# Attention with capped scores, then a two-way maxout layer, on one core: another hand-written order of the same steps, with three buffers for the exponentials instead of two

## The chip, the cores and the metric

The kernel runs on one core of one Trainium2 chip. The metric is the device time of one execution, in microseconds (us). TensorE (PE in the profile), ScalarE (ACT), VectorE (DVE), GpSimd (POOL) and SyncE (SP) each work through a queue of their own in order and wait for one another by semaphores. In this kernel POOL issues the loads that change type on the way, SP issues the transposing transfers and nearly all stores.

## The reference, cut to what matters

```python
# q, k, v: (8 batches, 12 heads, 448 rows, 64), float32; cap = 30
scores = scale * q @ k.T
scores = cap * tanh(scores / cap)
attn = exp(scores - max) / sum
x = (attn @ v), heads side by side        # (3584, 768)
out = maximum(x @ w1, x @ w2) @ w_out     # w1, w2: (768, 1024), w_out: (1024, 768)
```

The maximum is never taken directly: the kernel writes max(a, b) = b + relu(a - b), so with wd = w1 - w2 and wm = w2 @ w_out it computes out = x @ wm + relu(x @ wd) @ w_out.

## The kernel before, in words

**Tiles.** Two neighbouring heads of one batch are a pair of heads; there are 48 of them, and two of these make a *tile* t (0 to 23), four heads. An *item* n is what the attention works on at a time: a tile's 448 queries; tile 2 is cut in two (256 and 192 queries, items 2 and 3), so there are 25 items, and from tile 3 on item n is tile n - 1.

**The order is written out.** `ORDER` (line 10) is a string of 1911 steps. The kernel goes through it from first to last and issues what each step names (the table `STEPS`, line 686 on); every engine gets its share of the steps in that order. No planner decides at run time. A dependency between engines is a wait, which the framework derives from the tiles, so an engine runs ahead of the string wherever its own inputs allow. The steps that this document speaks of:

- `lk`, `lq`, `lv`, `lw1`, `lw2`, `lwo`: one load each on POOL's queue (of keys, queries, values, weights). Keys and queries of a tile go into one of four buffers `kqs`, values into one of four `vp` and `vl`.
- `X`, `XC`: for the first ten pairs of heads, TensorE transposes keys and queries and VectorE copies them to `qkT`. `cr t` does it for tiles 5 and up by one transposing transfer on SP's queue. `qkT` has three buffers, so a transfer also waits until an earlier tile's scores have been computed.
- `S n s z`: scores of item n, part s (0 to 5, 128 keys of two heads each), two matmuls into the score bank pair z (0 or 1). `L n z`: the scores of the 64 keys left over, eight matmuls. `T`, `TL`: tanh on ScalarE, from the bank pair to the exponentials' buffer. `E`: exp in place over two or three parts.
- `A`, `B`: VectorE adds up the exponentials; `Y`: TensorE sums them over the partitions; `Yi`: three VectorE steps to the reciprocal.
- `VL n z`, `V n u`: values times exponentials (8 and 12 matmuls, into bank pair z); `N`: VectorE normalizes into `xT`.
- `O g b` gives group g of the dense layers the bank b; `M x y c` makes c steps of it. With two different groups, a step is two matmuls of 64 rows each that run side by side on the two halves of the array (one half of x, the other half of y); with x = y it is one matmul of 128 rows; with -1 one half stands empty. Groups 0 to 11 are wm, the others belong to batches 0 to 7 in order. `H g` hands the bank from one half to the other by way of VectorE; `ev g` empties the bank to SBUF; `st` stores a block of the output. `sub` makes wd from w1 and w2 on VectorE.
- `D`: matmuls of a constant that nobody uses, which occupy TensorE at the start.

**The buffers of the exponentials.** An item has two tiles of them, one of 6 x 448 columns (`e0`) and one of 8 x 448 (`e1`). `exps_of` (lines 404 to 411) takes each from a pool of `EB` buffers, `EB = 2`. The tanh of item n + 2 can thus start only when the values and sums of item n have been read.

Places that the prediction uses: the first steps of `ORDER`; `lw1 2`, the last part of w1, and `sub 4`, which waits for it; `lv 2 1`, the second half of the values of tile 2; the transfers `cr 17` and `cr 20`; and the last item, 24, after which only dense groups 118 to 139 are left.

Of the kernel before, what the change touches and what calls it, by code (L numbers as in the profile page):

```python
# [14 lines left out]
lv 1 2; lq 6 0; lv 2 2; lw2 1; VL 0 1; W 2 2; WC 2; W 3 3; ev 1; WC 3; D 0 8; lq 5 0; E 0 1 0 2; E 0 0 0 3; Y 0 0;
Yi 0 1; Yi 0 2; Yi 0 3; lv 0 1; lv 0 0; lv 1 0; V 0 0; V 0 1; N 0 0; N 0 1; T 1 0; E 1 0 0 3; S 2 0 0; T 2 0;
E 1 1 2 4; E 1 1 0 2; O 2 2; O 3 1; M 2 3 8; H 3; H 2; lw2 2; W 4 3; WC 4; W 5 0; WC 5; M 3 2 3; lv 3 3; lk 5 0;
X 5 3; M 3 2 5; XC 5; S 2 1 0; lw1 0; sub 1 0; ev 3; L 2 1; TL 2; T 2 1; Y 1 0; Yi 1 1; Yi 1 2; sub 0 0; S 2 2 1;
T 2 2; E 2 1 0 2; O 4 3; O 5 1; M 4 5 8; H 5; lv 1 3; lv 1 1; VL 1 0; V 1 0; V 1 1; S 3 1 1; T 3 1; H 4; M 5 4 1;
ev 2; Yi 1 3; N 1 0; N 1 1; M 5 4 5; E 2 1 2 4; M 5 4 2; ev 5; S 3 0 1; T 3 0; lv 2 1; lq 8 0; lwo 1 0; O 6 0; O 7 2;  # L20
M 6 7 3; lk 6 0; M 6 7 1; lwo 1 1; M 6 7 2; S 3 2 0; T 3 2; M 6 7 2; H 7; H 6; ev 4; X 6 1; XC 6; L 3 1; TL 3;
E 3 1 0 2; lw1 1; sub 3 0; lk 10 0; lk 7 0; lv 3 2; lv 2 3; lv 2 0; lq 7 0; lk 8 0; lw1 2; lk 10 1; lq 10 0; lk 11 0;
lk 9 0; lk 11 1; lq 11 0; cr 5; lv 3 1; lq 9 0; lk 12 0; M 7 6 6; S 4 2 0; T 4 2; M 7 6 2; O 8 3; O 9 1; M 8 9 1;
ev 6; sub 2 0; ev 7; S 4 0 1; T 4 0; M 8 9 7; H 8; H 9; S 4 1 0; T 4 1; E 4 0 0 3; Y 2 0; Yi 2 1; Yi 2 2; VL 2 1;
X 7 2; XC 7; lk 12 1; lq 12 0; lk 13 0; lk 13 1; lq 13 0; lv 4 0; lv 4 1; lv 4 2; lv 4 3; lk 14 0; lv 3 0; lk 14 1;
lq 14 0; lk 15 0; lk 15 1; lq 15 0; X 8 0; XC 8; Yi 2 3; V 2 0; V 2 1; N 2 0; N 2 1; S 4 3 0; T 4 3; E 3 1 2 4;
M 9 8 8; ev 8; O 10 2; O 11 0; M 10 11 2; S 4 5 0; T 4 5; S 4 4 1; T 4 4; sub 5 0; M 10 11 6; H 11; H 10; sub 4 0;
ev 9; Y 3 3; Yi 3 1; S 5 2 0; T 5 2; M 11 10 4; S 5 0 1; T 5 0; M 11 10 4; Yi 3 2; ev 11; ev 10; L 4 0; TL 4; cr 6;
X 9 1; S 5 1 1; T 5 1; E 4 1 0 2; O 13 3; M 13 -1 2; O 14 0; M 13 14 4; O 17 2; M 17 14 2; XC 9; S 5 4 0; H 13;
M 17 13 3; H 14; M 17 13 1; M 14 13 2; VL 3 1; V 3 0; V 3 1; T 5 4; lv 5 0; lv 5 1; lv 5 2; lv 5 3; lk 16 0; lk 16 1;  # L30
lq 16 0; lk 17 0; lk 17 1; lq 17 0; lv 6 0; lv 6 1; lv 6 2; lv 6 3; lk 18 0; A 4 0 1; A 4 0 2; H 17; M 14 17 4; ev 13;
Yi 3 3; N 3 0; O 15 1; M 15 17 2; ev 17; O 19 3; M 15 19 4; H 15; N 3 1; E 4 1 2 4; L 5 0; TL 5; O 12 2; M 12 19 2;
H 19; M 12 15 4; H 12; M 19 15 2; ev 14; ev 15; A 4 1 1; S 5 3 1; T 5 3; E 5 1 0 2; M 19 12 4; ev 19; M -1 12 1;
O 18 0; M 18 12 1; O 16 1; M 18 16 5; H 18; M -1 16 1; H 16; S 5 5 0; cr 7; T 5 5; E 5 0 0 3; ev 12; M -1 18 1;
M 16 18 5; O 22 3; M 16 22 1; O 20 2; M 20 22 9; A 4 1 2; ev 18; B 4 0; B 4 1; L 6 1; VL 4 0; ev 16; A 5 1 1; Y 4 0;
Yi 4 1; Yi 4 2; Yi 4 3; V 4 0; V 4 1; TL 6; lk 18 1; lq 18 0; lk 19 0; lk 19 1; lq 19 0; lv 7 0; lv 7 1; lv 7 2;
lv 7 3; lk 20 0; M 20 22 4; H 22; O 21 1; M 20 21 1; H 20; M -1 21 1; N 4 0; N 4 1; M 22 21 4; A 5 0 1; S 6 5 1; cr 8;
M 22 21 8; H 21; S 6 1 0; M 22 20 2; M 21 20 2; E 5 1 2 4; A 5 1 2; A 5 0 2; ev 22; B 5 1; B 5 0; T 6 5; T 6 1;
S 6 4 1; T 6 4; M 21 20 4; S 6 0 0; T 6 0; E 6 1 2 4; M 21 20 6; ev 20; O 26 0; M 21 26 2; O 27 3; M 27 26 4; H 26;
S 6 2 1; S 6 3 0; T 6 2; T 6 3; E 6 0 0 3; ev 21; st 0 0; O 25 2; M 27 25 2; H 27; M 26 25 4; H 25; M 26 27 2; ev 26;  # L40
M 25 27 4; ev 27; O 29 1; M 25 29 2; ev 25; O 30 0; M 30 29 4; H 29; VL 5 1; Y 5 3; O 24 2; M 30 24 2; M 29 24 3;
S 7 5 0; M 29 24 1; H 30; M 29 30 2; V 5 0; V 5 1; T 7 5; lk 20 1; lq 20 0; lk 21 0; lk 21 1; lq 21 0; lv 8 0; lv 8 1;
lv 8 2; lv 8 3; lk 22 0; lk 22 1; lq 22 0; lk 23 0; lk 23 1; lq 23 0; Yi 5 1; Yi 5 2; Yi 5 3; H 24; M 24 30 3; ev 29;
N 5 0; M 24 30 1; ev 30; M 24 -1 1; O 31 3; M 24 31 1; O 28 1; M 28 31 1; ev 24; M 28 31 4; M 28 -1 1; H 28; H 31;
# [118 lines left out]
def kernel(  # L163
# [572 lines left out]
```

## Time and profile before

| what | us |
|---|---|
| three runs: median (lowest to highest) | 328.62 (328.51 to 330.5) |
| the profiled execution, its own time | 329.16 |
| its span, first to last instruction | 327.4 |
| TensorE busy | 319.1 |
| ScalarE busy | 274.5 |
| VectorE busy | 244.7 |
| GpSimd busy | 163.5 |

Busy time counts an engine's instructions, overlaps once. 1.76 us of the profiled execution lie outside of its span. In lines of the profile, `64*128` is a matmul on 64 rows and 128 columns of the array, `x24` a number of instructions, and a bracket is idle time of the engine just ahead, with what ended it.

### The profile page before, as it was taken

The numbers are of one execution on the slowest core, as the hardware profiler recorded it, in microseconds if no ns is written. First come the engines' busy times: TensorE is split into PE (matmuls) and PEld (weight loads), VectorE is DVE, ScalarE is ACT, GpSimd is POOL, SyncE is SP. The second block draws the span as 40 slices with busy tenths as digits, with TensorE's granted clock in tenths as the row PEclk, the third lists the DMA queues.
The fourth block names the chain that finished last, engine by engine and source line by source line (L and its number), as shares of the span: only waits on it lengthen the run. The fifth ranks groups of instructions, "written<-read, shape, count | busy, mean of one in ns | idle before, by whom it ended". The sixth has DMA issues, their size and how long they took to land.

```text
span 327.4 us, 10010 instructions
## 1 busy us (share of the span) xinstructions
PE 319.1 (97%) x4288; PEld 194.0 (59%) x4288; DVE 244.7 (75%) x447; ACT 274.5 (84%) x245; POOL 163.5 (50%) x241
## 2 busy tenths in 40 slices
PE   7799999999999999999999999999999999999995
PEld 7465567665546656555565565675567568555552
DVE  2349898988888688978888678889788777886213
ACT  3999999999999999999999998999899988900000
POOL 7567589998995865565577387543202000000000
PEclk9899999999999999999999999999999999999999
DMA  8999999999999999999999999996963006003034
GB/s 201 197 230 253 271 159 171 156 175 186 165 161 126 207 139 111 188 190 90 149 152 185 165 191 172 131 75 101 203 150 46 2 0 194 3 2 94 4 96 144
DMA packets 135083, 46.13 MB, mean 141 GB/s; under 512 B 116224, under 2 KB 130688, under 8 KB 134656
## 3 DMA queue, kind: packets, MB, share of 16 engines
q0 software_dynamic: 95168, 24.85, 76.9%
q1 hardware_dynamic: 39184, 19.40, 27.9%
q10 hardware_dynamic: 688, 1.25, 1.1%
q8 instruction: 33, 0.54, 0.7%
q14 instruction: 10, 0.08, 0.1%
HBM read 47.45 MB, written 11.01 MB: 179 GB/s over the span
## 4 chain that ended last, share of the span: by engine, by line
PE 94%; ACT 3%; DVE 2%; issue 0%; DVEq 0%
PE mm L582 59%; PE s L438 9%; PE s L539 9%; PE mm L577 8%; ACT e L447 2%; PE s L456 2%; PE s L529 2%; PE mm L502 2%; PE mm L336 2%; PE mm L365 1%; PE mm L497 1%; ACT e L469 0%; DVE xT L558 0%; PE mm L344 0%; ACT e L462 0%
## 5 line engine op out<-in xcount | busy, mean ns | idle before, releaser
L469 ACT ACTIVATE e<-e 128x1792 bf16<-128x1792 bf16 (+4 forms) x73 | 140.2, 1932 | 0.5
L447 ACT ACTIVATE e<-s 128x896 bf16<-128x896 f32 (+2 forms) x144 | 124.1, 935 | 6.0 <-PE s L438 5.7
L582 PE MATMUL mm<-wo_sb,gT 64*128 64x384 bf16 x768 | 95.8, 323 | 0.0
L582 PE MATMUL mm<-xT,wd_sb 64*128 64x448 bf16 (+2 forms) x768 | 79.9, 326 | 0.0
L582 PE MATMUL mm<-wm_sb,xT 64*128 64x384 bf16 x576 | 77.8, 323 | 0.0
L582 PEld LDWEIGHTS <-gT 64*128 64x128 bf16 x768 | 48.4, 94 | 23.3 <-issue 2.8
L302 POOL DMA_DIRECT2D vp<-in_v_dram x48 | 30.3, 637 | 60.6 <-PE s L539 29.0
L284 POOL DMA_DIRECT2D kqs<-in_k_dram x76 | 54.6, 721 | 9.7 <-DMA qkT<-kqs 3.1
L582 PEld LDWEIGHTS <-wd_sb 64*128 64x128 bf16 x768 | 46.3, 94 | 20.0 <-DVEq L590 2.4
L438 PE MATMUL s<-qkT 64*128 64x448 bf16 (+2 forms) x300 | 53.4, 346 | 2.6 <-ACT e L447 1.7
L582 PEld LDWEIGHTS <-xT 64*128 64x128 bf16 x576 | 38.2, 94 | 17.5 <-issue 2.2
L613 DVE TENSOR_SCALAR gT<-mm 128x448 bf16<-128x448 f32 (+2 forms) x72 | 38.9, 566 | 8.2 <-PE mm L582 4.4
L648 DVE COPY osb<-mm 128x384 f32<-128x384 f32 x54 | 28.4, 551 | 15.8 <-PE mm L577 11.5
L284 POOL DMA_DIRECT2D kqs<-in_q_dram x38 | 35.0, 921 | 1.5 <-DMA vl<-in_v_dram 0.7
L539 PE MATMUL s<-e,vp 128*32 128x448 bf16 (+2 forms) x600 | 32.1, 346 | 0.0
L558 DVE TENSOR_TENSOR xT<-s,inv 64x448 bf16<-64x448 f32 (+2 forms) x50 | 30.2, 603 | 2.4 <-PE mm L582 0.9
L479 DVE TENSOR_TENSOR esum<-esum,e 128x896 bf16<-128x896 bf16 x42 | 25.5, 618 | 7.8 <-PE mm L582 6.9
L438 PEld LDWEIGHTS <-qkT 64*128 64x128 bf16 x300 | 20.2, 94 | 18.6 <-issue 6.8
L302 POOL DMA_DIRECT2D vl<-in_v_dram x48 | 29.4, 622 | 0.3 <-DMA wo_sb<-in_moe_w_out_dram 0.3
L484 DVE TENSOR_TENSOR esum<-esum,e 64x896 bf16<-64x896 bf16 x42 | 26.0, 619 | 3.1 <-PE mm L582 0.8
L479 DVE TENSOR_TENSOR esum<-e 128x896 bf16<-128x896 bf16 x42 | 25.4, 617 | 2.9 <-PE mm L582 1.8
L509 DVE STREAM_TRANSPOSE st<-mm 128x448 f32<-128x448 f32 (+2 forms) x25 | 15.8, 630 | 13.3 <-PE mm L502 10.8
(54 smaller groups left out, 262.1 us busy)
## 6 DMA issues: line engine op xcount, KB each, us to landing
out_dram<-osb SPq DMA_DIRECT2D x51, 192.0 KB, 3.7
vp<-in_v_dram POOLq DMA_DIRECT2D x38, 160.0 KB, 4.9
kqs<-in_q_dram POOLq DMA_DIRECT2D x46, 112.0 KB, 4.9
kqs<-in_k_dram POOLq DMA_DIRECT2D x76, 56.0 KB, 4.3
osb<-in_moe_w_dram POOLq DMA_DIRECT2D x2, 1024.0 KB, 8.3
gT<-in_moe_w_dram POOLq DMA_DIRECT2D x3, 512.0 KB, 7.2
wo_sb<-in_moe_w_out_dram POOLq DMA_DIRECT2D x4, 384.0 KB, 7.0
w1l<-in_moe_w_dram POOLq DMA_DIRECT2D x1, 1024.0 KB, 5.2
```

Of the source, the lines that this page charges most:

```text
L284: nc.gpsimd.dma_start(out=to, in_=x)
L302: nc.gpsimd.dma_start(out=to, in_=x)
L438: nc.tensor.matmul(ps[:, h, x * w : (x + 1) * w], k_of(t, o, h, j), q_of(n, o, h))
L447: nc.scalar.activation(e, slots[n, s][:, :, :m], AF.Tanh, scale=scale / cap)
L469: nc.scalar.activation(e[:, j0 * m : hi], e[:, j0 * m : hi], AF.Exp, scale=float(cap))
L479: nc.vector.tensor_add(d, e[:, 0:2, :] if j == 1 else d, e[:, 2 * j : 2 * j + 2, :])
L539: nc.tensor.matmul(vals[n][R32[m], u, :w], vp[t % VB][:, x, j if turned_by_pe(t) else 2 * j, u::2], e_of(n, o, h, j), start=False, stop=(j ...
L558: nc.vector.tensor_mul(x[to], vals[n][r, 1, :w], sums[n, 3][to, :w])
L577: nc.tensor.matmul(self.ps, w, x, start=first, stop=self.at[0] == self.n)
L582: ins = nc.tensor.matmul(self.ps, w[r], x[r], start=first, stop=self.at == [self.n, self.n]).ins
L613: nc.vector.tensor_relu(gT[b // 2][:, f, cs], ps)
L648: nc.vector.tensor_copy(o[:, hs], ps)
```

## The change

`EB` is 3 instead of 2, and `ORDER` is another string, of 1910 steps. Nothing else differs: every kind of step occurs as often as before, for the same items, groups and loads, but for `M`, whose 1324 steps are cut into 406 pieces instead of 407. Of these steps 1140 are pairs, 160 full and 24 single in both. What differs is the place of nearly every step. The diff, cut to the lines that the prediction speaks of:

```diff
 ORDER = """
-ld0 k; ld0 q; ld1 k; ld1 q; lq 3 0; dm; D 0 32; D 0 8; ms0; cd k; lk 3 0; lw2 0; id; lv 0 3; lv 0 2; cd q; Xh 0 1 0;
-XC 0 1; cd1 q; Xh 0 0 1; XC 0 0; S 0 0 0; T 0 0; S 0 1 1; T 0 1; X 3 2; S 0 2 0; cd1 k; X 1 3; T 0 2; XC 3; S 1 3 1;
...
-ev 2; Yi 1 3; N 1 0; N 1 1; M 5 4 5; E 2 1 2 4; M 5 4 2; ev 5; S 3 0 1; T 3 0; lv 2 1; lq 8 0; lwo 1 0; O 6 0; O 7 2;
...
-M 121 -1 2; ev 121; H 118; ev 123; lv 23 1; lv 23 2; lv 23 3; VL 24 0; V 24 0; Y 24 0; Yi 24 1; Yi 24 2; V 24 1;
...
+ld0 k; ld0 q; ld1 k; dm; D 0 32; ms0; lk 5 0; ld1 q; lq 3 0; lq 4 0; lq 2 0; cd q; cd1 q; cd k; id; Xh 0 0 0; XC 0 0;
+Xh 0 1 1; XC 0 1; S 0 1 0; T 0 1; S 0 0 1; T 0 0; S 0 2 0; T 0 2; E 0 0 0 3; cd1 k; X 1 2; D 3 8; XC 1; S 0 3 1;
+T 0 3; S 0 4 0; T 0 4; E 0 1 0 2; D 3 8; lk 3 0; X 3 3; XC 3; ms; lk 2 0; X 2 0; S 0 5 1; T 0 5; S 1 5 0; T 1 5;
+lw2 0; W 0 1; W 1 2; XC 2; WC 0; L 0 1; TL 0; L 1 0; TL 1; lk 4 0; X 4 3; S 1 1 1; T 1 1; WC 1; lwo 0 0; O 0 0; O 1 1;
...
+sub 3 0; S 4 2 1; T 4 2; E 4 0 0 3; M 9 8 8; ev 8; lk 10 1; lq 8 0; lk 7 0; lk 8 0; X 8 2; XC 8; X 7 0; ev 9; lw1 2;
+sub 4 0; lq 10 0; lk 11 0; lv 2 1; lk 11 1; lq 11 0; cr 5; lk 9 0; lq 9 0; Y 2 3; Yi 2 1; XC 7; S 5 0 0; T 5 0;
+S 5 2 1; T 5 2; O 10 2; O 11 1; M 10 11 8; H 10; Yi 2 2; VL 2 0; V 2 0; V 2 1; H 11; Yi 2 3; N 2 0; N 2 1; A 4 0 1;
...
+lv 15 0; lv 15 1; lv 15 2; S 17 4 0; T 17 4; lv 15 3; lk 36 0; lk 36 1; lq 36 0; lk 37 0; lk 37 1; lq 37 0; cr 18;
+lv 16 0; lv 16 1; lv 16 2; lv 16 3; M 82 74 2; H 75; M 75 74 1; B 16 0; M 75 74 6; cr 17; L 18 1; TL 18; E 17 0 0 3;
...
+lk 41 1; lq 41 0; cr 20; lv 18 0; lv 18 1; lv 18 2; lv 18 3; st 3 4; st 3 5; A 18 0 2; ev 92; lk 42 0; lk 42 1;
...
+O 122 1; M 118 122 2; M 121 122 12; TL 24; E 24 1 2 4; B 24 0; A 24 1 2; VL 24 0; V 24 0; H 118; B 24 1; N 23 1;
...
-    EB = 2
+    EB = 3
```

More of the change, by code (lines that the diff above doesn't have):

```diff
@@ L15 @@
[L15 to L19, printed above, removed]
@@ L20 @@
-ev 2; Yi 1 3; N 1 0; N 1 1; M 5 4 5; E 2 1 2 4; M 5 4 2; ev 5; S 3 0 1; T 3 0; lv 2 1; lq 8 0; lwo 1 0; O 6 0; O 7 2;
[L21 to L44, printed above, removed]
@@ L158 @@
+O 138 1; M 138 138 2; st 7 4; ev 137; ev 136; st 7 5; st 7 3; M 138 138 12; ev 138; O 139 0; M 139 139 14; ev 139;
 st 7 6;
```

251 lines of the change are left out of this document (136 added, 115 removed).

## The prediction

> **What bounds the kernel now.** I read the page first, for the engines' shares, their slices and the chain.
>
> ```profile
> span 327.4 us, 10010 instructions
> ...
> PE 319.1 (97%) x4288; PEld 194.0 (59%) x4288; DVE 244.7 (75%) x447; ACT 274.5 (84%) x245; POOL 163.5 (50%) x241
> ...
> PE   7799999999999999999999999999999999999995
> ...
> ACT  3999999999999999999999998999899988900000
> ...
> DMA  8999999999999999999999999996963006003034
> ...
> PE 94%; ACT 3%; DVE 2%; issue 0%; DVEq 0%
> ```
>
> TensorE is busy 97% of the span and makes up 94% of the chain; ScalarE is nearly as full until slice 36. The reader should see two full engines and a short thin start. Next, the windows by stage (engine busy us, granted clock, DMA):
>
> ```profile
> core 0: us, PE busy (x) PEld busy (x) DVE busy (x) ACT busy (x) POOL busy (x), PEclk, DMA share, GB/s
> 0.00:5.00 5.00, 4.01 (x38) 4.01 (x39) 0.58 (x3) 1.85 (x2) 3.90 (x11) 1.00 0.65 193
> 5.00:10.00 5.00, 3.68 (x97) 2.43 (x94) 2.27 (x5) 3.17 (x5) 3.16 (x6) 1.00 1.21 199
> 10.00:15.00 5.00, 3.54 (x44) 1.75 (x46) 0.69 (x1) 5.00 (x6) 3.77 (x8) 0.81 1.29 201
> 15.00:20.00 5.00, 4.48 (x83) 2.69 (x79) 1.69 (x6) 5.00 (x7) 2.95 (x6) 0.84 1.27 200
> 20.00:26.00 6.00, 5.94 (x98) 4.08 (x100) 4.31 (x8) 5.97 (x4) 4.32 (x8) 1.00 1.15 295
> 26.00:60.00 34.00, 33.91 (x646) 22.05 (x644) 30.55 (x57) 33.50 (x33) 26.52 (x39) 1.00 1.47 201
> ...
> 283.40:327.40 44.00, 40.20 (x338) 22.41 (x338) 22.12 (x41) 2.58 (x3) 0.00 (x0) 1.00 0.22 63
> ```
>
> From 26 to 283 us TensorE is never idle; its idle time lies in the first 20 us (4.3 us of it) and in the last wait for stores. In 10 to 20 us ScalarE has no gap, so there TensorE follows ScalarE. The granted clock is 0.81 and 0.84 there. Then the waits, and two pieces of the timeline: the first score, and a change from one matmul shape to another.
>
> ```profile
> POOL vp L302 <- PE s L539: 29.0, 6, 8.2
> ...
> ACT e L447 <- PE s L438: 5.7, 9, 1.5
> ...
> PE s L438 <- ACT e L447: 1.7, 5, 0.4
> ...
> ACT e L462 <- PE s L539: 0.3, 1, 0.3
> ```
> ```profile
> 5.56 0.83 PEld L365 LDWEIGHTS <-kqs 64*64 64x64 bf16 x28 [0.39 <-issue]
> ...
> 6.99 0.55 PE L438 MATMUL s<-qkT 64*128 64x448 bf16 x4 [0.49 <-DVE qkT L370]
> 7.39 4.96 ACT L447 ACTIVATE e<-s 128x896 bf16<-128x896 f32 x6 [1.54 <-PE s L438]
> ```
> ```profile
> 139.76 0.37 PE L502 MATMUL mm<-esum,ones 128*32 128x448 bf16 x4
> 139.95 1.32 PE L539 MATMUL s<-e,vp 128*32 128x448 bf16 x24
> 141.20 0.33 PE L582 MATMUL mm<-wm_sb,xT 64*128 64x384 bf16 x1
> ```
>
> TensorE waits for ScalarE 1.7 us in all. ScalarE's tanh begins at 7.39 us, and what it waited for is the first score, which waited for a copy to `qkT`, which waited behind filler matmuls: operands were cast by 4.83 us, but the first transpose starts at 5.59. In the last piece, the 24 `V` matmuls start at 139.95 and the next pair at 141.20: 1.25 us, where two `V` back to back cost 2 x 0.57.
>
> **The change part by part.** No engine gets an instruction more or less: counting the steps gives the same matmuls, exps, adds, 237 POOL steps with their loads and 72 SP transfers. So the time can change only by waits, and by what stands next to what.
>
> *How I lay the order out.* In the trace of before, each TensorE step's start-to-start time is: `S` 0.189 us, `L` 0.21, `V` 0.57, `VL` 0.305, `Y` 0.195, a pair step 0.162 or 0.189 (384 or 448 columns), `X` 0.56. End to end this gives 306.0 us for either order. In before, the real start of a step is later than this sum by an offset: 8.0 us at 20.5 us, 8.8 at 38, 17.6 at the end. What the change does is what it does to the offset.
>
> *The start.* The change moves the filler `D 0 8` from ahead of the first transpose to behind the third score, and transposes the keys first. Before: filler until 5.44, transpose 5.59, score 6.99, tanh 7.39. After: keys cast at 4.47, 32 fillers done at 4.6, transposes at 4.6 and 4.97 (queries cast at 4.83), copies by 6.0, score 6.05, tanh 6.45. ScalarE starts 0.94 us earlier. It then runs without a gap (0.80 us a tanh, 1.59 and 2.34 an exp); walking it to the value step of item 0 puts that at about 22.7 us at 16.2 us of work, an offset of 6.5 where before has 7.9. POOL issues four small loads before the identity instead of three, 0.6 us, which ends at 4.05 and is hidden by the cast. I take 0.9 off, the lead of ScalarE, since the two engines stay tied; ends: 0 (eaten later) and 1.4 (the offset).
>
> *Changes of shape.* Between 64*128 work and the 128*32 or 64*32 steps, the trace loses 0.09 to 0.12 us each time (median 0.105); between `VL`, `Y` and `V` 0.01. I count 81 such costly changes before and 72 after, mostly because the sums stand between two `V` now. The difference is 5 in the waiting start, 3 in the stretch to about 130 us where ScalarE decides, and 2 after. I take those 2: 0.2 off; ends 0 and 9 x 0.105 = 0.95. The Trainium skill, page "TensorEngine Tiling (Array Packing)", section "Tiling Modes", says that a change of tiling mode drains the engine; the trace agrees for the costly ones with its 0.105 us and not for those at 0.01, and by that rule all nine would pay: 0.95 off here, 327.1 in the end.
>
> *The third buffer.* ScalarE waited once for values to be read, 0.3 us. So the buffer itself saves 0 to 0.3; I take 0. It makes legal what the new order does, such as the tanh of item 12 ahead of the values of item 10.
>
> *Waits in the middle.* I laid ScalarE and VectorE out against TensorE's steps in the same way (`A` 0.54, `B` 0.64, `N` 0.64 + 1.29, `Yi` 0.68 + 0.28 + 0.65, an `ev` 0.48 or 0.54). For before this meets the trace within 0.4 us. For after the nearest covers are short by 0.28 us (hand-over `H 13` on VectorE, 52 us, behind `ev 11` and `sub 5`), 0.24 (`VL 1` for the tanh `T 3 1`) and 0.15 (`VL 0`); all else holds by 0 to 0.3. Shifts are not added, as one also moves what follows. I charge 0.3; ends 0 and 1.0.
>
> *Loads on POOL's queue.* Order and issue times by position: `lv 2 1`, half the values of tile 2, moves from 26th load to 40th, beside `lk 11 0`, which in before issues at 39.19 and lands at 44.87. The loads ahead of it are the same less three small ones, so it lands at about 44.9; `V 2 0` stands at 38.05 us of work, so at 45.5: 0.6 us to spare. `lw1 2` (37th instead of 39th) lands at about 42, and `sub 4`, behind which VectorE has `Yi 2 1`, `XC 7` and the hand-over that `M 11 10` needs, stands at 43.0. `lk 9`, `lq 9` land at about 47.3, `X 9` stands at 47.7. Later loads run 40 us ahead in both orders: POOL's waits for `vp` (29.0 us) are waits for buffers. I charge 0; ends 0 and what rival 2 gives.
>
> *Transfers on SP's queue.*
>
> ```profile
> L373 SPq DMA_TRANSPOSE qkT<-kqs x19: 1296/1787/4352, 46.6 to 242.4; - x19
> ...
> DMA to landing us min/median/max: 3.4/6.4/10.6
> ```
>
> `cr` needs a free `qkT`, and everything ahead of it on SP. In before a transfer takes the buffer that comes free first (`cr 13` at 132.16, when tile 10 was done, tile 11 not). For after the tightest is `cr 17`: buffer free at 183.3, first use at 195.2; less 6.4 or 10.6 to land, 5.5 or 1.3 us stay. `cr 20` takes the buffer of tile 17 (206.9, use 224.3). Those behind stores, `cr 9` and `cr 15`, can issue at 87.6 and 159.5 and are used at 104.2 and 173.5. Charge 0.
>
> *The end.* Work from `VL 24` on is 31.5 us after, 31.1 before; ScalarE's last exp ended at 286.0 against 292.0, and by my layout comes 2.4 us later now, still covered. 0.
>
> Sum: -0.9 - 0.2 + 0.3 = -0.8. The profiled execution took 329.16 (span 327.4 and 1.76 around it), which gives 328.4 against its own time; it stands 0.54 above the median of 328.62, so I predict 327.8.
>
> **The rivals.** *1. The clock takes the start back.* Within the window of 10 to 15 us the clock is 0.81, and a finer cut shows 0.50 for 14 to 16. It fell after a stretch in which TensorE only followed ScalarE, and cost little, as TensorE waited anyway. The new order leaves TensorE as thin from 11.6 to 16.2 us (about 2 us of work), then wants 2.6 us of pair steps. If half of the clock falls on these, half of that, 1.3 us, is lost: -0.8 + 1.3, 329.1. For: the same thinness. Against: two fillers of 8 now stand at 8 to 10.4 us. The Trainium skill, page "TensorE: Matmul & The Clock Gate", section "Part 1: The HAM clock gate", says that the clock halves after an idle window of about 3.4 us and recovers after a busy one; the 0.50 in the trace agrees, though TensorE was not fully idle. By that rule the fall would come again, and the time would be this rival's.
>
> *2. Slower: values that land late.* `V 2 0` heads TensorE's queue with 0.6 us to spare before `lv 2 1`. It decides from a landing at 45.5 on, and every us later is one of TensorE, since nothing behind it can pass. A landing as slow as the slowest transfer of the loads, 10.6 us after issue instead of 5.7, is 4.9 later: 49.8, or 4.3 lost: 332.1. For: the DMA digits are 8 and 9 there and POOL waits for landings (3.5, 2.4, 1.8 us). Against: those waits are earlier, and the same bytes stand ahead.
>
> *3. Faster.* The offset of 1.4 stays, all nine changes of shape count, covers hold, and of the small losses of before (its offset grows by 8.8 us from 38 us on, of which about 72 x 0.105 = 7.6 are shape) another 1.2 goes: -3.5, 325.1. Against: ScalarE has 0.1 us of idle time in 60 to 120, so TensorE can't run away from it.
>
> *4. It makes no difference:* ScalarE, tied to TensorE at several places by 0 to 0.2 us, gives the lead back in waits: 328.6.
>
> **How the numbers follow.** Forecast 0.40, rival 1 0.18, rival 2 with milder forms of late transfers 0.18, rival 3 0.12, rival 4 0.12. Slower by over 1% (about what a measurement here can tell from no change; 331.9) is rival 2 but for its mild forms, 0.16; faster (325.3) is rival 3, 0.12; the rest, 0.72, within 1%. The range goes from 325.3 to 331.2, which leaves out rival 3's end and the full rival 2; the forecast's own is 327.0 to 328.6.
>
> **What would show it.** First tanh at 6.4 to 6.6 us; `VL 0` at about 22.7; no TensorE gap over 0.3 us from 26 us on; TensorE's busy time within 1 us of 319.1. Wrong if a `V` of item 2 or `X 9` waits for a DMA near 45 to 48 us, if a score waits for `qkT` near 195 us, or if the clock is under 0.9 in 17 to 20 us.

## The result, and the profile after

The changed kernel took 330.7 us (median of 20 executions), the kernel before 329.33 (20 executions on the same chips): a ratio of 1.0045, with a 95% interval of 1.0027 to 1.0064. The change made the kernel about 0.45% slower, where I had forecast 0.8 us less. The ratio leaves out the two longest of the twenty (334.38 and 334.41 us). The profiled execution took 331.83 us, with a span of 330.0. First its page, in the lines that answer to those of before:

```profile
span 330.0 us, 10010 instructions
...
PE 319.4 (97%) x4288; PEld 199.2 (60%) x4288; DVE 245.9 (74%) x447; ACT 274.8 (83%) x245; POOL 163.1 (49%) x241
...
PE   7899999999997999999999999999999999999995
...
ACT  4999999999999899999999998999899977820000
...
DMA  8999999999999999999999999996694014004014
...
PE 69%; DMA 14%; ACT 10%; POOL 4%; issue 1%; DVE 0%; POOLq 0%
```

TensorE is busy 0.3 us longer than before (319.1), so 2.3 of the 2.6 us by which the span grew are waiting. One digit shows it: the 7 in slice 13, near 105 us. The chain shows more: TensorE made up 94% of it before and makes up 69% now, and 14% are DMA, which was not in it at all. The windows by stage, from 0 to 120 us (columns as in the prediction):

```profile
0.00:5.00 5.00, 3.86 (x43) 3.62 (x45) 0.58 (x3) 1.85 (x2) 3.91 (x12) 1.00 0.65 200
5.00:10.00 5.00, 3.88 (x69) 2.63 (x63) 1.69 (x4) 3.76 (x5) 4.77 (x8) 1.00 1.14 177
10.00:15.00 5.00, 4.94 (x90) 3.59 (x88) 1.82 (x7) 4.97 (x4) 1.32 (x3) 1.00 1.21 198
15.00:20.00 5.00, 3.71 (x73) 2.24 (x73) 1.62 (x3) 5.00 (x8) 1.36 (x3) 1.00 1.30 201
20.00:26.00 6.00, 6.00 (x99) 3.75 (x97) 4.20 (x8) 6.00 (x6) 5.58 (x10) 1.00 1.26 178
26.00:60.00 34.00, 32.95 (x627) 20.96 (x625) 29.01 (x54) 32.09 (x31) 22.33 (x34) 1.00 1.34 209
60.00:120.00 60.00, 57.87 (x823) 34.88 (x819) 49.16 (x92) 58.51 (x52) 44.47 (x64) 1.00 1.61 147
```

The first 26 us are better than before, and the clock did not fall in this execution. Then TensorE idles 1.05 us from 26 to 60 us, where it idled 0.09, and 2.1 us from 60 to 120, where it idled none. The waits name what it and VectorE waited for:

```profile
POOL vp L302 <- PE s L539: 21.1, 5, 9.1
...
ACT e L447 <- PE s L438: 9.6, 16, 1.4
...
PE s L456 <- DMA qkT<-kqs: 1.7, 1, 1.7
DVE wd_sb L323 <- DMA osb<-in_moe_w_dram: 1.7, 1, 1.7
...
DVE wd_sb L323 <- DMA w1l<-in_moe_w_dram: 0.8, 1, 0.8
```

The last three lines are new: a score waits for a transfer (`cr 9`), and VectorE's subtractions `sub` wait for the parts of w1, with everything queued on VectorE behind them (evictions, hand-overs, normalizing). The first line fell from 29.0 to 21.1 us: POOL waits less for free `vp`, which fits loads that run later. The start of TensorE and ScalarE, from the timeline:

```profile
4.74 0.95 PE L365 MATMUL mm<-ident,kqs 64*64 64x64 bf16 x28
...
6.18 0.93 PE L438 MATMUL s<-qkT 64*128 64x448 bf16 x4 [0.48 <-DVE qkT L370]
...
6.77 1.73 ACT L447 ACTIVATE e<-s 128x896 bf16<-128x896 f32 x2 [0.98 <-PE s L438]
```

The first tanh is at 6.77 us, 0.62 earlier than before. The piece that answers to the change of shapes:

```profile
198.97 0.75 PE L539 MATMUL s<-e,vp 128*32 128x448 bf16 x12
199.55 0.36 PE L502 MATMUL mm<-esum,ones 128*32 128x448 bf16 x4
199.74 0.74 PE L539 MATMUL s<-e,vp 128*32 128x448 bf16 x12
200.41 0.50 PE L582 MATMUL mm<-wo_sb,gT 64*128 64x384 bf16 x4
```

The sum `Y` stands between the two `V` here and costs no change: start to start 0.58 and 0.19, and 0.67 at the one step back to a pair. Last the transfers `cr`, on SP's queue, and the score that waited (two views of one kernel, the second cut to one place):

```profile
L373 SPq DMA_TRANSPOSE qkT<-kqs x19: 1296/1737/6210, 49.0 to 244.9; - x19
...
DMA to landing us min/median/max: 3.4/6.3/15.4
```
```profile
89.05 2.50 SPq L629 DMA_DIRECT2D out_dram<-osb  x4
91.85 12.32 SPq L373 DMA_TRANSPOSE qkT<-kqs  x2
```
```profile
105.15 0.38 PE L529 MATMUL s<-e,vl 64*32 64x448 bf16 x8
107.28 0.38 PE L456 MATMUL s<-qkT 64*32 64x448 bf16 x8 [1.74 <-DMA qkT<-kqs]
```

SP issues four stores, and behind them `cr 9` at 91.85 us. It lands at 107.24, 15.4 us later; the longest landing before was 10.6. The score that heads TensorE's queue loses 1.74 us.

**Where the time went, in one measure.** For every profile I took each TensorE step's start less the sum of the steps ahead of it (lengths as in the prediction, but fillers counted as nothing, since orders with more of them are compared). The number at 16 us of work is what the start cost; its growth from 22 to 58 us is what the stretch of the loads cost; its growth from 58 to 298 us is the rest. For before it is 13.48, 1.81 and 6.83; for after 12.66, 3.64 and 8.35. So the start gave 0.8, close to what I charged, and 1.8 went in the loads' stretch and 1.5 behind it, where `cr 9` alone cost 1.74. The profiled execution of after is 1.1 us above its median, so these are the parts of one execution and not yet those of the 0.45%.

The landing times of the loads, taken from the trace and set against the first step that needs them, say which loads these are:

```
load      lands  needed   to spare    |  before: to spare
lw1 0     32.15  32.17    0.02        |  1.55
lwo 1 1   37.01  M 6 waits 0.5 for it |  2.5
lw1 1     40.74  40.84    0.10        |  2.78
lw1 2     46.20  46.22    0.02        |  over 3
lv 2 1    47.69  47.73    0.04        |  over 3
lq 9      49.98  50.20    0.22        |  over 3
lv 3 3    61.87  62.15    0.28        |  over 3
lv 2 3    21.52  46.94   25.4         |
lv 2 2    24.41  46.94   22.5         |
```

Where 0.02 or 0.04 us are left, the engine had been waiting and went on with the landing: VectorE 1.73 us for `lw1 0` and 0.83 for `lw1 2` (the waits above), TensorE 0.48 for `lv 2 1`:

```profile
47.73 0.84 PE L539 MATMUL s<-e,vp 128*32 128x256 bf16 x24 [0.48 <-DMA vp<-in_v_dram]
```

At 0.10 us and more (`lw1 1`, `lq 9`, `lv 3 3`) no wait of VectorE or of a matmul ended with the landing. The last two rows stand ahead of `lw1 0` in POOL's queue and are needed 15 us after it.

### The profile page after: what moved, and what is told of

It reads as the page before. It is cut to its first block, busy times and chain, and to the rows that moved or that the text cites. A ratio compares the mean times of both kernels' runs of the same rounds, so it can differ in the third digit from the quotient of the medians.

```text
span 330.0 us, 10010 instructions
## 1 busy us (share of the span) xinstructions
PE 319.4 (97%) x4288; PEld 199.2 (60%) x4288; DVE 245.9 (74%) x447; ACT 274.8 (83%) x245; POOL 163.1 (49%) x241
## 3 DMA queue, kind: packets, MB, share of 16 engines
q10 hardware_dynamic: 688, 1.25, 1.0%
## 4 chain that ended last, share of the span: by engine, by line
PE 69%; DMA 14%; ACT 10%; POOL 4%; issue 1%; DVE 0%; POOLq 0%
PE mm L582 44%; PE mm L577 8%; PE s L539 7%; PE s L438 6%; DMA qkT<-kqs 5%; ACT e L469 5%; ACT e L447 4%; DMA osb<-in_moe_w_dram 4%; DMA gT<-in_moe_w_dram 4%; DMA vp<-in_v_dram 2%; POOL kqs L277 2%; PE s L456 2%; PE s L529 1%; PE mm L502 1%; ACT e L462 1%
## 5 line engine op out<-in xcount | busy, mean ns | idle before, releaser
L447 ACT ACTIVATE e<-s 128x896 bf16<-128x896 f32 (+1 forms) x144 | 124.7, 942 | 10.0 <-PE s L438 9.6
L582 PE MATMUL mm<-xT,wd_sb 64*128 64x448 bf16 (+2 forms) x768 | 78.9, 326 | 0.0
L582 PE MATMUL mm<-wm_sb,xT 64*128 64x384 bf16 x576 | 78.8, 323 | 0.0
L582 PEld LDWEIGHTS <-wd_sb 64*128 64x128 bf16 x768 | 49.0, 94 | 18.2 <-DVEq L590 2.3
L438 PE MATMUL s<-qkT 64*128 64x448 bf16 (+2 forms) x300 | 54.2, 350 | 1.4 <-DVE qkT L370 0.7
L302 POOL DMA_DIRECT2D vp<-in_v_dram x48 | 30.3, 638 | 43.5 <-PE s L539 21.1
L582 PEld LDWEIGHTS <-xT 64*128 64x128 bf16 x576 | 39.1, 94 | 16.3 <-issue 1.3
L539 PE MATMUL s<-e,vp 128*32 128x448 bf16 (+2 forms) x600 | 33.0, 346 | 0.5 <-DMA vp<-in_v_dram 0.5
L438 PEld LDWEIGHTS <-qkT 64*128 64x128 bf16 x300 | 20.4, 94 | 14.9 <-issue 5.2
## 6 DMA issues: line engine op xcount, KB each, us to landing
osb<-in_moe_w_dram POOLq DMA_DIRECT2D x2, 1024.0 KB, 10.2
```

Source lines behind the costliest of these rows:

```text
L302: nc.gpsimd.dma_start(out=to, in_=x)
L438: nc.tensor.matmul(ps[:, h, x * w : (x + 1) * w], k_of(t, o, h, j), q_of(n, o, h))
L447: nc.scalar.activation(e, slots[n, s][:, :, :m], AF.Tanh, scale=scale / cap)
L539: nc.tensor.matmul(vals[n][R32[m], u, :w], vp[t % VB][:, x, j if turned_by_pe(t) else 2 * j, u::2], e_of(n, o, h, j), start=False, stop=(j ...
L582: ins = nc.tensor.matmul(self.ps, w[r], x[r], start=first, stop=self.at == [self.n, self.n]).ins
```

## The experiments

Theory: the new order is good for what its start promises, but it loads in the wrong order for its own pace, so TensorE, VectorE and `cr 9` wait for transfers. Rivals: the third buffer costs by itself; ScalarE gives any gain back; the clock does. All runs in one table, with the offset as above (us); "ratio" is to the kernel before on the same chip in the same session. It is not the ratio of the medians: before's own median was 328.90 beside e1 to e4, 329.02 beside e5 to e8, 329.10 beside e9 to e12, 329.14 beside e13 to e15 and 329.11 beside e16 and e17.

| run | kernel, edit | median us | ratio, 95% interval | at 16 | 22 to 58 | 58 to 298 |
|---|---|---|---|---|---|---|
| | before | 329.33 | 1 | 13.48 | 1.81 | 6.83 |
| | after | 330.7 | 1.0045, 1.0027 to 1.0064 | 12.66 | 3.64 | 8.35 |
| e1 | after, cr 9 ahead of stores | 330.15 | 1.0035, 1.0015 to 1.0054 | 14.78 | 2.20 | 6.84 |
| e2 | after, four loads earlier | 330.6 | 1.0058, 1.0032 to 1.0084 | 12.21 | 4.28 | 6.82 |
| e3 | e1 and e2 | 331.05 | 1.0065, 1.0046 to 1.0084 | 13.04 | 4.66 | 6.83 |
| e4 | before, EB = 3 | 328.89 | 1.0002, 0.9984 to 1.0020 | 14.86 | 1.69 | 6.74 |
| e5 | after, 30 loads by use | 330.19 | 1.0037, 1.0013 to 1.0061 | 12.47 | 2.21 | 8.62 |
| e6 | e5 and e1 | 329.72 | 1.0019, 1.0002 to 1.0037 | 14.66 | 2.38 | 6.60 |
| e7 | before, filler later | 329.59 | 1.0013, 1.0000 to 1.0025 | 14.26 | 1.81 | 6.64 |
| e8 | after, filler earlier | 332.86 | 1.0100, 1.0054 to 1.0146 | 13.92 | 2.21 | 8.83 |
| e9 | e6 and more fillers | 330.54 | 1.0051, 1.0024 to 1.0078 | 12.62 | 5.95 | 6.60 |
| e10 | after, more fillers | 330.95 | 1.0036, 1.0015 to 1.0057 | 12.32 | 5.38 | 7.18 |
| e12 | e1 and more fillers | 330.96 | 1.0050, 1.0035 to 1.0065 | 13.02 | 4.17 | 6.73 |
| e11 | before, more fillers | 329.75 | 1.0017, 1.0005 to 1.0029 | 14.09 | 1.81 | 6.84 |
| e13 | e9, loads by use up to lv 3 3 | 328.72 | 0.9975, 0.9957 to 0.9993 | 12.50 | 2.22 | 6.89 |
| e14 | e13 without more fillers | 328.77 | 0.9988, 0.9963 to 1.0013 | 12.66 | 2.21 | 6.89 |
| e15 | e13, exp behind tanh | 328.59 | 0.9968, 0.9947 to 0.9989 | 12.14 | 2.07 | 6.90 |
| e16 | after, only loads by use up to lv 3 3 | 329.79 | 1.0010, 0.9985 to 1.0035 | 12.21 | 2.21 | 6.89 |
| e17 | e15, cr 9 behind stores | 328.77 | 0.9988, 0.9972 to 1.0005 | 12.18 | 2.07 | 6.89 |

An offset is that of one profiled execution; times are medians of 5 to 20.

### e1 to e4: one suspect each

e1:

```diff
-st 0 1; st 0 0; cr 9;
+cr 9; st 0 1; st 0 0;
```

> The changed kernel with one step moved: the transfer cr 9 stands ahead of the stores st 0 1 and st 0 0 instead of behind them. In the profile of the changed kernel these stores wait for ev 23, are issued at 89.1 us, cr 9 behind them at 91.9 and lands at 107.2, where the score that needs it loses 1.7 to 1.8 us. Theory (late transfers ate the gain): cr 9 issues as soon as its buffer is free, lands in time, the gap at 105 us is gone, and the time falls by 1.0 to 1.8 us against the changed kernel, to about 329.1 to 329.7, no slower than before. Rival (the gap at 105 us only stands in the profiled execution, or what is gained there is waited for again at the next tie to ScalarE): less than 0.5 us.

Measured: `cr 9` issued at 82.4 us and landed 7.4 us later, 16 us ahead of its use, and the last column fell to before's 6.84. So its place behind the stores was the cause of that wait. The median fell by less than I said: it stands 1.25 us above that of before, where after stood 1.37 above its own, and the interval overlaps that of after; in the medians that is the rival's case. This execution started late, as the clock fell (below).

e2: `lw2 0` behind `lk 5 0`, `lv 2 1` ahead of `lv 1 3`, `lv 3 2; lv 3 3` behind `lv 1 1`, in POOL's queue alone.

> The changed kernel with early loads moved on POOL's queue only: lw2 0 two places earlier in time (behind lk 5), lv 2 1 ahead of lv 1 3, lv 3 2 and lv 3 3 ahead of the loads behind lv 1 1. Theory (late loads cost the 30 to 60 us stretch): the values of item 2 and of item 3 land before V 2 0 and VL 4 want them, the gaps of 0.55 us at 47 us and of 0.57 us at 61 us are gone, and the time falls by about 1.0 us against the changed kernel (0.5 to 1.4). Rival (the loads share one stream of transfers, so that another load becomes the late one; or the loss of that stretch is ScalarE's and VectorE's): within 0.4 us of the changed kernel, with new gaps of the same sum between 26 and 62 us.

The rival's case. `lv 2 1` was early now, but `lw1 0` landed at 33.27, `lwo 1 1` at 37.97 and `lw1 1` at 41.48, about 1 us later than in after, and the stretch lost 4.28. What is moved ahead delays all behind it.

e3: both edits. e4: `EB = 3` in the kernel before.

> Both moves together: cr 9 ahead of the stores, and the early loads moved. Theory: the two losses lie at different places and add up: 2 to 3 us below the changed kernel, about 327.5 to 328.7, below the kernel before by 0.5 to 1.5 us. Rival (one tie to ScalarE behind both places takes the gain back): not below the kernel before.

> The kernel before with EB = 3 and its own order: only the third buffer of the exponentials. Theory: 0 to 0.3 us faster, within 0.3 us of the kernel before, as ScalarE waited 0.3 us for a buffer. Rival (the buffer itself costs, by where the tiles come to lie in memory or by more to wait for): 0.5 us or more slower than before, the same loss as the whole change.

e3 was not below the kernel before, as its rival said, but for another reason: with the `cr 9` wait gone, 4.66 us were lost at the loads. e4 settles the third buffer in the order of before: no difference.

### e5 to e8: the loads in order of use, and the start

e5, shown by the sequence on POOL's queue (the places between other steps stay):

```diff
-lw2 1; lv 1 0; lv 0 1; lv 0 0; lv 0 2; lv 0 3; lv 2 3; lw2 2; lv 1 3; lv 2 2; lv 1 2; lv 2 0; lv 1 1; lq 5; lk 6; lw1 0;
-lk 10 0; lwo 1 0; lwo 1 1; lq 6; lq 7; lw1 1; lk 10 1; lq 8; lk 7; lk 8; lw1 2; lq 10; lk 11 0; lv 2 1;
+lw2 1; lv 0 1; lv 0 0; lv 0 2; lv 0 3; lw2 2; lw1 0; lq 5; lwo 1 0; lwo 1 1; lv 1 3; lv 1 2; lv 1 0; lv 1 1; lk 6; lq 6;
+lw1 1; lk 8; lq 8; lk 7; lq 7; lw1 2; lv 2 2; lv 2 3; lv 2 0; lv 2 1; lk 10 0; lk 10 1; lq 10; lk 11 0;
```

> The changed kernel with 30 early loads of POOL's queue (from lw2 1 to lv 2 1) put in the order in which their data are used; nothing else moves. In the profile of the changed kernel lw1 0, lw1 1, lw1 2, lwo 1 1, lv 2 1 and lq 9 land 0.0 to 0.2 us ahead of their use, while lw2 2, lv 2 2, lv 2 3 and lv 2 0, loaded before, land 22 to 25 us ahead of it; the kernel before has 1.5 us or more at each part of w1. Theory (the new order of loads makes the 30 to 60 us stretch wait): lw1 0 lands by about 30, lwo 1 1 by 35 and lw1 1 by 39 us, no subtraction waits for a DMA, TensorE's sum of gaps from 26 to 62 us falls by 1.0 to 1.4 us and the time by 0.8 to 1.4 us against the changed kernel, to about 1.000 to 1.002 of before. Rival (the transfers together are the limit, so order doesn't matter): ratio stays at 1.003 to 1.006.

> The same reordered loads, and cr 9 ahead of the stores st 0 1 and st 0 0. Theory: as the run with the loads alone, and without the executions that lose 1.8 us at cr 9 (five of the twenty timed runs of the changed kernel took 332.5 us or more): median lower by 0 to 0.5 us again, none above 332. Rival: no difference to the run with the loads alone.

(Of the loads that the first expectation calls early, `lw2 2` is not one: TensorE's transposes `W 5 0` use it at 26.74 us in after, 2.7 us behind its landing.) In both profiles the stretch lost 2.2 to 2.4 us instead of 3.6, and no subtraction waited for a DMA. In e5 `cr 9` landed 15.6 us after issue and cost 2 us; in e6 it did not. The theory holds for the places; for the time it does not: e5's ratio of 1.0037 lies where its rival put it. The medians stand 1.17 and 0.70 us above that of before in the same session, where after stood 1.37 above its own, and the intervals overlap with after's. What was missing shows in e6's first column, 14.66. Its windows, and those of e5, which had no such loss:

```profile
10.00:15.00 5.00, 2.91 (x78) 2.33 (x77) 2.60 (x8) 4.97 (x5) 1.32 (x3) 1.00 1.20 196
15.00:20.00 5.00, 4.17 (x58) 2.09 (x59) 0.93 (x2) 3.89 (x5) 1.07 (x2) 0.52 1.27 206
20.00:26.00 6.00, 6.00 (x80) 3.19 (x78) 2.35 (x4) 5.22 (x6) 3.93 (x6) 0.83 1.10 295
```
```profile
10.00:15.00 5.00, 3.10 (x82) 2.44 (x80) 2.42 (x8) 4.97 (x5) 1.20 (x3) 1.00 1.23 195
15.00:20.00 5.00, 3.79 (x73) 2.35 (x74) 1.12 (x2) 5.00 (x7) 1.67 (x3) 1.00 1.28 209
20.00:26.00 6.00, 6.00 (x99) 3.70 (x96) 4.38 (x9) 6.00 (x7) 3.47 (x7) 1.00 1.09 292
```

The two kernels differ by `cr 9` alone, which comes behind 80 us: with the clock at half from 15.2 to 22.0 us ScalarE itself runs dry (3.89 of 5 us busy), and 2.2 us are lost. So the clock is a draw of each execution, not of the order alone.

e7 and e8 move one filler:

```diff
 (e7, before)  -D 0 32; D 0 8;   +D 0 32;      -X 1 3; T 0 2;   +X 1 3; D 0 8; T 0 2;
 (e8, after)   -dm; D 0 32;      +dm; D 0 32; D 0 8;      -X 1 2; D 3 8; XC 1;   +X 1 2; XC 1;
```

> The kernel before with one step moved: the filler D 0 8 stands behind X 1 3 instead of ahead of the first transposes. Theory (the start is worth what I charged where the loads leave room, as in the order before, with 1.1 us or more at every load): first tanh at 6.7 to 6.8 us instead of 7.4 and the time lower by 0.4 to 0.7 us, ratio 0.998 to 0.999. Rival 1 (a start gain is eaten by the clock, whose half-speed window then falls later, as in the run with EB = 3 alone, which lost 1.3 us to a fall at 17.0 instead of 13.2 us): no gain or up to 1 us slower. Rival 2 (ScalarE, tied at later places, gives it back): no change.

> The changed kernel with one step moved back: the first filler of eight stands ahead of the first transposes, as before. First tanh about 0.6 us later, at 7.3 us. Theory (late loads hold this order between 26 and 62 us, so an earlier start buys nothing): time within 0.3 us of the changed kernel, and the offset at the first dense group of the second half of w_out is the same. Rival (the start carries through to the end): 0.6 us slower than the changed kernel, ratio 1.006 to 1.007.

Both came out other than the theory said. e7's first tanh was 0.49 us earlier, and the kernel not faster (14.26 at 16 us of work). e8's first tanh did not come later, 6.46, and the kernel was the slowest of all. The timelines show what became of the start, e7 first, then e8:

```profile
4.86 0.96 PE L365 MATMUL mm<-ident,kqs 64*64 64x64 bf16 x28 [0.28 <-ACT kqs L264]
...
7.16 0.96 PE L365 MATMUL mm<-ident,kqs 64*64 64x64 bf16 x28
```
```profile
3.83 0.89 PE L336 MATMUL mm<-warm 128*128 128x128 bf16 x13
4.87 0.63 PE L365 MATMUL mm<-ident,kqs 64*64 64x64 bf16 x28
```

The 28 transposes of a pair take 0.96 us in e7, and 0.63 in e8. TensorE begins at half its rate (fillers 0.107 us apart in e8, and 0.056 from 3.8 us on). Full rate came at 3.8 us in e8, so that its filler was done when the keys were cast, and at 9.9 in e7, whose transposes were longer by 0.33 us a pair, which fits that it lost what it had won. In the profiles with `D 0 8` in front full rate came by 6.8 us (4 of 4), without it as late as 9.9 to 13.3 us in 3 of 15; that the filler in front brings it on is likely, but not shown by so few. In e8, which has a filler less in the middle, the clock fell from 17.5 to 20.9 us, and `cr 9` cost 2.3 us. By its three columns the profiled execution is only 0.3 us behind that of after; why the six timed ones lie higher is not shown.

### e9 to e12: keeping the clock up

The fillers that are added, in e9, e10 and e12 at the first six places, in e11 at nine others:

```diff
+behind Xh 0 1 1: D 3 6   S 0 0 1: D 3 8   X 2 0: D 1 16   S 0 5 1: D 1 10   W 1 2: D 3 20   L 0 1: D 3 9
```

> The changed kernel with reordered early loads and cr 9 ahead of the stores, and with filler matmuls in the six places between 5.5 and 17 us where TensorE waited (6, 8, 16, 10, 20 and 9 of them, 0.056 us each at full clock, 0.107 at half). Theory (what is left to the kernel before is the clock: the profiled execution without the fillers fell to half from 15.2 to 22.0 us and lost 2.2 us, and its four timed executions with a recorded mean of 1.0 all took 328.75 to 328.78): with TensorE kept busy the clock no longer falls, nearly all executions come to 328.3 to 329.0, ratio 0.997 to 0.999. Rival 1 (the fillers stand in ScalarE's way, at half clock above all): 329.5 to 330.5. Rival 2 (the falls have another cause): as without the fillers, 329.7 with executions up to 332.

> The changed kernel with only the same fillers: loads and cr 9 stay as they are. Theory: the clock's share of the loss goes and the share of late loads and of cr 9 stays: 0.4 to 1.0 us below the changed kernel, ratio 1.001 to 1.003, with single executions still 2 us longer by cr 9. Rival (a start without falls is held up by the loads anyway): ratio stays at 1.0045.

> The changed kernel with the fillers and cr 9 ahead of the stores, the early loads as they are. Theory: between the two others, 1.0 to 1.4 us above the run that has all three (the late loads' part when the clock stays up), none above 331.5. Rival (late loads cost nothing in the timed executions): equal to the run that has all three.

> The kernel before with filler matmuls in the nine places between 9.4 and 17.2 us where TensorE waited (4 to 9 of them each). Theory: its clock falls too (all three profiles of this order fell, at 13.2, 13.3 and 17.0 us, the last one 1.35 us dearer), and eight of 27 timed executions took 330.2 us or more where the others took 328.2 to 329.1; with fillers the upper group is gone, all at 328.3 to 329.0, and the median moves by less than 0.3 us. Rival (the upper group has another cause): it stays, one execution in three.

The clock stayed up to 60 us in all four profiles. Yet e9 rose to 1.0051: that theory of what was left fell. Its offset at 16 us, 12.6, is low, but the stretch of the loads lost 5.95 us. Windows and timeline of e9:

```profile
26.00:60.00 34.00, 33.74 (x638) 21.79 (x634) 30.00 (x56) 32.74 (x31) 22.28 (x35) 1.00 1.33 179
60.00:120.00 60.00, 58.26 (x803) 35.12 (x803) 47.84 (x90) 57.16 (x52) 53.34 (x75) 0.97 1.60 166
```
```profile
61.19 0.35 PE L529 MATMUL s<-e,vl 64*32 64x448 bf16 x1 [0.35 <-ACT e L447]
62.88 0.38 PE L529 MATMUL s<-e,vl 64*32 64x448 bf16 x7 [1.35 <-DMA vl<-in_v_dram]
```

`VL 4 1` was there at 61.19 and had to wait for `lv 3 3`, which landed at 62.84; the clock then fell for 3.4 us (63.8 to 67.2). At half clock that is worth up to 1.7 us, an estimate, so not all of the 5.95 is waiting for loads. I had put only the loads up to `lv 2 1` in order. A TensorE that starts earlier runs into the next late load. e10 and e12 lost 5.4 and 4.2 us in that stretch without such a fall; their intervals can't be told apart from those of e9 or of after. e10's 1.0036 lies between its theory and its rival, and e12 came out equal to e9, as its rival said, and not 1.0 us above it. In e11 the upper group of before (330.2 us and more) was gone, as said, but so was the lower one: 329.1 to 330.0. As 4 of the 28 executions of before beside e11 were in that group, eleven executions without it are weak evidence. By the profiles (14.09 at 16 us of work against 13.48) the fillers cost the old order more than its fall at 13.2 us does.

### e13 to e17: all loads in order of use

e13: as e9, with the sequence of e5 continued, `cr 5` and `cr 6` behind their loads:

```diff
-lk 10 0; lk 10 1; lq 10; lk 11 0; lk 11 1; lq 11; cr 5; lk 9; lq 9; ... lk 12 0; ... lv 4 1; cr 6; ... lv 3 2; lv 3 1; lv 3 0; lv 4 2; lv 4 3; lk 14 0; lv 3 3;
+lk 9; lq 9; lk 10 0; lk 10 1; lq 10; lk 11 0; lk 11 1; lq 11; cr 5; ... lv 3 2; lv 3 3; lv 3 0; lv 3 1; lk 12 0; ... lq 13; cr 6; ... lv 4 0; ... lv 4 3; lk 14 0;
```

> The changed kernel with the fillers, cr 9 ahead of the stores, and all loads from lw2 1 to lv 3 3 in the order of use (lk 9, lq 9 and the values of item 4 now early too; cr 5 and cr 6 stand behind their loads). In the earlier run with fillers TensorE stood at 12.6 us of offset at 16 us of work, earlier than any profile of the kernel before (13.5 to 14.9), but lost 6.0 us from 22 to 58 us of work where the kernel before loses 1.8: V 4 waited for lv 3 3 (landing 62.8), X 9 for lq 9. Theory (late loads are the whole of it): that stretch loses 2.2 to 2.6 us, no wait for a load above 0.2 us; time 328.3 to 329.0 in most executions, ratio 0.997 to 1.000. Rival (the queue as a whole can't deliver by then, whatever the order): other loads become late, the stretch still loses 3.5 us or more, ratio 1.003 to 1.006.

> The same without the fillers. Theory: executions in which the clock stays up at 328.7, those in which it falls between 15 and 22 us 0.5 to 2.5 us longer; median 0.3 to 0.8 us above the run with fillers, ratio 1.001 to 1.002. Rival (the queue as a whole is the limit, and a later start only hides it): at or below the run with fillers.

> The run with fillers and reordered loads, with one step of ScalarE moved: E 5 1 0 2 behind T 5 1 instead of ahead of it, so that VL 4 1 finds its bank pair read 1.6 us earlier. In every profile of this order VL 4 1 waits 0.46 us for that tanh. Theory: the gap ahead of VL 4 1 falls from 0.57 to 0.11 us and the time by 0.2 to 0.46 us. Rival (ScalarE gives it back at its next tie): no change to the run without this move.

e13 gave what the theory said: 2.22 us in the stretch, no load late, and 0.9975 of before. Between e9 and e13 only the places of loads differ (`cr 5` and `cr 6` stand behind their own in both), and their intervals lie apart (1.0024 to 1.0078, and 0.9957 to 0.9993). That is the strongest single proof. Two more pairs differ by the loads alone: e12 and e13 (1.0035 to 1.0065 for e12), and, without the fillers, e1 and e14 (1.0015 to 1.0054, and 0.9963 to 1.0013). e14, without fillers, is not to be told from e13 by its ratio, which is lower than the 1.001 to 1.002 that I had said; its executions spread from 328.1 to 331.0, those of e13 from 328.4 to 329.5, which fits that the fillers take away the dear falls of the clock. e15's edit:

```diff
-T 5 3; E 5 1 0 2; ... T 5 1;
+T 5 3; ... T 5 1; E 5 1 0 2;
```

In after, `VL 4 1` waits for a tanh that ScalarE does behind that exp; in e15 it doesn't (after, then e15):

```profile
61.09 0.71 PE L582 MATMUL mm<-wo_sb,gT 64*128 64x384 bf16 x6
62.15 0.38 PE L529 MATMUL s<-e,vl 64*32 64x448 bf16 x8 [0.35 <-ACT e L447]
```
```profile
59.77 0.38 PE L529 MATMUL s<-e,vl 64*32 64x448 bf16 x8
60.09 0.75 PE L539 MATMUL s<-e,vp 128*32 128x448 bf16 x12
```

The wait is gone, but e15 and e13 can't be told apart by their times. By the offsets 0.15 of the 0.46 us was kept (2.22 to 2.07), so the rival was right for most of it. e15 beats both kernels; its median is 0.55 us below that of before. Its windows, to be held against those of after:

```profile
10.00:15.00 5.00, 4.98 (x118) 4.35 (x116) 2.74 (x8) 4.97 (x5) 1.65 (x3) 1.00 1.21 194
...
20.00:26.00 6.00, 6.00 (x99) 3.58 (x96) 4.71 (x9) 6.00 (x7) 3.92 (x6) 1.00 1.10 294
26.00:60.00 34.00, 34.00 (x647) 21.95 (x642) 30.53 (x57) 33.20 (x32) 26.41 (x40) 1.00 1.38 184
60.00:120.00 60.00, 59.84 (x845) 35.92 (x839) 51.04 (x95) 59.90 (x54) 51.99 (x74) 1.00 1.76 171
```

TensorE is full from 26 to 60 us, though fewer bytes a second move there than in after (184 against 209 GB/s): more has come earlier, with 294 against 178 GB/s in 20 to 26 us.

> The changed kernel with all loads from lw2 1 to lv 3 3 in the order of use, and nothing else: cr 9 behind the stores, no more fillers. Theory: the stretch from 22 to 58 us of work loses 2.2 to 2.6 us instead of 3.6, so ratio 1.000 to 1.003, with executions 1.8 to 2.3 us longer where cr 9 lands late. Rival (cr 9 behind the stores costs nothing in the timed executions, and the profiles that showed it were the exception): equal to the run that has the loads and cr 9 moved, 0.9988.

> The run with everything (loads in order of use, fillers, the exp of item 5 behind its tanh), but cr 9 behind the stores again, as in the changed kernel. In profiles of this order with that place cr 9 cost 1.8, 2.0, 2.3, 0.7 and 0 us. Theory: median 0.7 to 2.0 us above the run with everything, ratio 0.999 to 1.003. Rival: no difference, ratio 0.997.

e16 is the changed kernel with its loads in order, nothing else: 1.0010, about level with before; its interval overlaps that of after a little. That is where its theory had it, and its longest executions, 331.0 to 334.0, fit a late `cr 9`. In both profiles `cr 9` stood behind the stores and cost nothing: it landed 12.6 and 10.2 us after issue, at 102.8 and 101.6, with 0.9 and 2.0 us to spare. In the five other profiles with it behind the stores it took 13.2 to 15.8 us (after, e2, e5, e8, e10), and cost 0 to 2.3. So that place makes it late enough to be at the mercy of the traffic; why it was 3 us faster in these two is not settled. e17 against e15 leaves its cost in the medians open, as the intervals overlap. The longest executions tell more. Six pairs of runs differ by the place of `cr 9` alone (after and e1, e2 and e3, e5 and e6, e10 and e12, e16 and e14, e17 and e15): with it behind the stores 12 of 77 executions took 332.5 us or more, with it ahead none of 59.

## Why the prediction was wrong

- **The start, -0.9:** right in size, by -0.8 in the profile (13.48 to 12.66). That this size came out rests on one profile of each kernel: other profiles of after's order, without more fillers, have 12.2 to 14.8 at 16 us of work, by where the clock falls. I took the tanh to come at 6.45 and `VL 0` at 22.7; the tanh came at 6.77 (6.10 to 6.98 in profiles of this order, as the rate of the first matmuls differs from execution to execution), `VL 0` at 23.38. That moving the filler makes the start is not shown: in e7 it brought the tanh forward without a gain, in e8 it did not delay it.
- **Changes of shape, -0.2:** behind 58 us of work the growth was 6.83 before and 6.60 to 6.90 in new orders without a wait at `cr 9`. The 0.2 is too small to see in that. The 0.95 of the rule is not tested by it, since most of the changes lie ahead of 58 us or near it; my three parts, 5, 3 and 2, also make ten and not nine.
- **The third buffer, 0:** right in the order of before (e4).
- **Waits in the middle, +0.3:** near in size, wrong in place. Without late loads the stretch loses 2.2 us, 0.4 more than before. The cover that was short by the most was not among the three that I named: `VL 4 1` waits 0.46 us for a tanh, which my layout had held to be covered.
- **Loads on POOL's queue, 0: this is the step that failed.** I looked at `lw1 2`, `lv 2 1` and X 9's loads, and let "Later loads run 40 us ahead in both orders" stand for the rest. I did not look at `lw1 0`, `lw1 1` and `lwo 1 1`, whose slack in before was 1.6 to 2.8 us and which moved back in the queue (`lw1 0` is issued at 24.35 instead of 19.84), nor at `lv 3 3`. And those I did look at came later than I estimated: `lv 2 1` 47.7 for 44.9, `lw1 2` 46.2 for 42, `lq 9` 50.0 for 47.3. I took landing times from before and shifted them by what stood ahead, as if a place in the queue were a time. What the sequence changed shows in 20 to 26 us, where 178 GB/s moved in after, 295 in before and 294 in e15; POOL's own standing still does not tell them apart (busy 2.7 of the 10 us from 10 to 20 in after, 2.8 in e15). The price in the profile was 3.64 - 2.21 = 1.4 us, and 3.2 where TensorE came earlier (e10). It is no term beside the start: e1 and e8, with the loads of after and a start made late by a fall of the clock, lost only 2.2 us in the stretch. The first two columns add up to 16.3 in after, 17.0 in e1 and 16.1 in e8, and to 14.2 to 14.9 in e5 and e13 to e17. With the loads where they are, an early start is waited away.
- **Transfers on SP's queue, 0:** failed too. "Those behind stores, `cr 9`" was named with an issue at 87.6 and a use at 104.2, and 10.6 us as the longest landing: 6 us to spare. It was issued at 91.85, because the stores ahead of it waited for `ev 23`, and took 15.4 us. 1.7 us in the profile.
- **Rival 1, the clock:** it did not happen in the profile of after, but does in others of the same order (e1, e6: 14.7 to 14.8 at 16 us of work instead of 12.2 to 12.7). Its price, put at 1.3, is about 2.2 us there (e6 against e5). That it is a part of why the median lies above what the best executions reach is likely, but no run separates it.
- **Rival 2, late values:** its mechanism is the one that decided, by other loads first: not one load at 4.3 us, but seven with at most 0.3 us to spare, four of which were waited for. I gave it 0.18. Its price rested on 10.6 us as the slowest load; in before that was a transfer, `cr 13`, and the slowest load took 8.9 us. In after loads took up to 13.0. The signs that I named for "wrong" (a `V` of item 2 waiting for a DMA near 47 us) came true.

How the 0.45% divide among loads, `cr 9` and the clock in the timed executions is not settled: single edits (e1, e5) have intervals that overlap with after's. That the loads cost time is shown by three pairs (e9 and e13, e12 and e13, e1 and e14), that `cr 9` behind the stores makes long executions by the count above. That the two together take the loss away is shown by e14: 0.9988, with an interval apart from after's. The 0.8 us of the forecast would be 0.9976. That lies within e14's interval as 1 does, so the rest of the sum is neither shown nor refuted.

## What to carry to other kernels

When an order is changed, list every load with the time at which it lands and the step that first needs it, in the old and the new place, and look first at those with the least to spare; in this queue, loads put ahead of their need delayed those behind them by about 1 us (e2). Sorting the loads by first use moved the time about as much as the whole change had (0.45%): 0.47% from e1 to e14, 0.76% from e9 to e13, and 0.35%, with intervals that overlap, from after to e16. A gain at the start is worth only as much as the next transfer leaves of it, as e9's profile shows: 2.0 us ahead of e6's at 16 us of work, 1.5 us behind it at the end, with the fall of the clock behind its wait as a part of that.

## What the runs showed of the hardware that I had not expected

- The window of 0 to 5 us says a clock of 1.00 in each of these profiles, yet the 28 transposes near 4.8 us took 0.95 or 0.96 us in after and e7 and 0.63 in e8. Ahead of the first recorded change (13.3 us in after) the row can't be trusted; the length of a known matmul can.
- Falls of the clock were recorded as stretches of 3.4 or 6.8 us (13.15 to 16.56 in before, 15.2 to 22.0 in e6), at another place in each execution of one order. The offset at 16 us of work was 1.4 us higher where a fall of 3.4 us began at 17.0 us than at 13.2 (e4 and before, which share the order; one profile of each). The Trainium skill, page "TensorE: Matmul & The Clock Gate", section "Part 1: The HAM clock gate", says that the window is free-running and about 3.4 us long; the trace agrees, 3.41 and twice that. Cut into such windows from the first recorded change on, the 19 traces show what came ahead of a fall: in each of the ten falls that came before TensorE's work was done, TensorE had been busy 50 to 56% of the window before, and of some 1700 other windows at full clock only four lie below 57%. e9's fall at 63.8 us fits that: its wait for `lv 3 3` lies in the window before.
- `cr 9` landed 5.8 to 7.4 us after issue in the profiles of this order where it stood ahead of the stores, and 10.2 to 15.8 us behind them, while SP's own part in issuing it grew from 1.5 to 2.3 us to 3.2 to 5.6.
